# A new written-out order for an attention-then-mixer kernel, with half the scores of six more head pairs masked in SBUF

## The chip, the cores and the metric

The kernel runs on one core of one Trainium2 chip. A core has a matrix engine (TensorE, PE in the profile), a vector engine (VectorE, DVE), a scalar engine (ScalarE, ACT), GpSimd (POOL), and SyncE (SP), which here only issues transfers. Each engine works through its own list of instructions in the order in which they were written, and waits on semaphores for the others. Matmuls write to PSUM, which has eight banks; everything else lies in SBUF. The metric is the device time of one execution in microseconds.

## What is computed

The reference has two parts. The first is linear attention with a decay per head, over 4 batches, 8 heads, 768 positions and head size 64. It goes in blocks of 64 positions:

```
intra = (q_block @ k_block.T) * Dmask          # Dmask[i, j] = lam**(...) for i >= j, else 0
out   = intra @ v_block + (q_block * lam_pow) @ kv_state
kv_state = lam**64 * kv_state + (k_block * rev_pow).T @ v_block
```

The second part takes the heads side by side as x (4 x 768 x 512) and mixes the tokens:

```
W_tok = (x @ w_q) @ (x @ w_k).T / sqrt(64)     # per batch, 768 x 768
out   = relu(W_tok @ x) @ w_out
```

## The kernel before, in words

**Tiles.** Heads go two at a time: a *pair* n is batch n // 4 and heads 2(n % 4) and 2(n % 4) + 1, so there are 16 pairs, four to a batch. Positions go in six chunks of 128. All data are bf16 on the chip; the inputs are f32 in memory and are cast by the load.

**Pieces of a pair.** Each pair passes through a fixed set of pieces. On TensorE: `Aq` and `Ak` turn q and k by 12 transposes each (L251, L260); `S0` and `S1` make the scores of chunks 0 to 2 and 3 to 5 (six matmuls each, L277); `P` makes the running sums of k times v (10, L319); `I` multiplies q by these (10, L347) and `V` adds scores times v (12, L359), both into the same two banks; `F` turns the result (six, L382). Between them stand copies out of PSUM: `eq` (VectorE, also multiplies by the decay, L266), `ek`, `G`, `ex` and `ef`, each on ScalarE or VectorE as the order says (L234; `G` of pairs from 6 on is three VectorE instructions, L335 to L337). `sv` multiplies v by its decay, in SBUF, on VectorE or GpSimd (L239).

**Masks.** The scores have to be multiplied by a mask of ones and zeros. `M0` and `M1` (L291) do this on VectorE straight out of PSUM. For half the scores of pairs 0 to 3 the old order has two steps instead: `Mc` (L306) copies the unmasked scores to SBUF on ScalarE, and `Mm` (L310) multiplies them there by the mask, on VectorE, both operands lying in SBUF.

**Pieces of a batch.** Once the four `ef` of a batch b are there: `Q` (two halves, L404; for batch 0 in eight parts `Qp`, L414), `eQ`, `K` (L430; `Kh` in batch 0), `eK`, `Y` (L455), the three copies `YA`, `YB`, `YC` out of one bank, four `m` (two matmuls each, L479), their relu copies `em` (or halves, `eh`, L490 on ScalarE and L492 on VectorE), and six `O` (four matmuls of 512 columns, L508) with copies `eo`, each followed by a store of 256 KB that SyncE issues (L519). `Z` are matmuls on zeros that nobody reads (L528).

**What sets the order.** No scheduler runs when the kernel is built. A text, `ORDER`, names the pieces one after the other, and a loop at the end (L540) issues them. A word such as `ek.5@1:v` is piece `ek` of pair 5 on PSUM bank 1, on VectorE (`:a` ScalarE, `:p` GpSimd). Pieces with two banks use the named one and the next. So one text fixes the list of every engine, and the bank of every piece; a piece that writes a bank waits until the copy that read the bank's previous contents is done. GpSimd's list holds the loads of q, k and v, one pair after another, with nine of the sixteen `sv` between them. `hold` makes SyncE wait for k of pair 14 before its first store.

The text was found by a search that planned with costs and landing times; the search itself is not part of the kernel. The loop that issues it:

Of the kernel before, what the change touches and what calls it, by code (L numbers as in the profile page):

```python
# [28 lines left out]
ORDER = """  # L29
q.2 k.2 v.2 q.3 k.3 v.3 wq.0 wk.0 q.4 k.4 v.4 wo.0 q.5 k.5 v.5 q.6 k.6 v.6 q.7 k.7 v.7 sv.4:p q.8  # L30
k.8 v.8 sv.5:p q.9 k.9 v.9 q.10 k.10 v.10 sv.7:p q.11 k.11 v.11 q.12 k.12 v.12 sv.9:p q.13 k.13
v.13 sv.10:p q.14 k.14 v.14 sv.11:p q.15 k.15 v.15 sv.12:p sv.13:p sv.14:p hold.14 Aq.0@0 dq.2
eq.0@0 dq.3 Z.5@7 Ak.0@0 dq.1 ek.0@0:v Z.3@7 S1.0@0 sv.0:v S0.0@2 Mc.0@2 M1.0@0 Z.3@7 P.0@4 Aq.1@5
G.0@4:a Mm.0:v Z.1@7 I.0@0 eq.1@5 Ak.1@4 V.0@0 ek.1@4:v ex.0@0:a S0.1@4 sv.1:v S1.1@2 Mc.1@4 Z.1@7
F.0@0 M1.1@2 P.1@1 ef.0@0:a Aq.2@4 Mm.1:v G.1@1:a eq.2@4 Z.1@7 Ak.2@0 I.1@2 ek.2@0:v V.1@2 S1.2@0
sv.2:v ex.1@2:a S0.2@4 Mc.2@4 M1.2@0 Z.3@7 P.2@2 Aq.3@3 G.2@2:a Mm.2:v F.1@4 eq.3@3 Ak.3@2
ef.1@4:v I.2@0 V.2@0 ek.3@2:v ex.2@0:a sv.3:v Z.1@7 S0.3@2 S1.3@4 cw.0:a M1.3@4 Mc.3@2 Z.2@7 P.3@0
Qp.0.0@1 F.2@6 G.3@0:a Mm.3:v Qp.0.1@1 ef.2@6:a I.3@4 V.3@4 Qp.1.0@0 ex.3@4:a Aq.4@6 Ak.4@7 eq.4@6
F.3@4 ek.4@7:a Qp.1.1@0 Qp.0.2@1 eg.3.0@4:v Qp.1.2@0 eg.3.1@4:v Qp.0.3@1 eQ.0.0@1:v Qp.1.3@0
S1.4@4 eQ.0.1@0:a Kh.0.0@1 M1.4@4 ek2.0.0@1:a Kh.0.1@0 S0.4@6 ek2.0.1@0:a M0.4@6 Y.0@0 YA.0@0:a  # L40
YB.0@0:v Aq.5@1 YC.0@0:a m.0.1@6@7 eq.5@1 m.0.0@4@5 eh.0.1.0@6:a eh.0.0.0@4:v eh.0.0.1@5:a Ak.5@1
eh.0.1.1@7:a m.0.2@4@6 ek.5@1:v m.0.3@5@0 eh.0.2.1@6:a eh.0.3.1@0:v S0.5@2 eh.0.3.0@5:a S1.5@6
eh.0.2.0@4:v P.4@0 O.0.5@5 G.4@0:v M1.5@6 I.4@0 eo.0.5@5:a V.4@0 M0.5@2 Aq.6@4 ex.4@0:a Ak.6@5
eq.6@4 O.0.4@6 ek.6@5:a sv.6:v S1.6@4 S0.6@0 M1.6@4 F.4@7 O.0.3@2 ef.4@7:a M0.6@0 P.5@3 eo.0.3@2:a
Ak.7@7 G.5@3:v Aq.7@0 ek.7@7:a P.6@2 eq.7@0 I.5@4 V.5@4 G.6@2:v S0.7@0 ex.5@4:a eo.0.4@6:v Aq.8@7
M0.7@0 I.6@2 S1.7@4 O.0.0@6 eq.8@7 M1.7@4 V.6@2 eo.0.0@6:a O.0.2@7 ex.6@2:a sv.8:v P.7@6
eo.0.2@7:a Ak.8@2 G.7@6:v P.8@3 ek.8@2:a F.5@7 G.8@3:v Aq.9@6 ef.5@7:a Ak.9@2 eq.9@6 S1.8@4
ek.9@2:a S0.8@0 I.7@6 M1.8@4 V.7@6 F.6@2 ex.7@6:a M0.8@0 O.0.1@3 ef.6@2:v F.7@6 eo.0.1@3:a Aq.10@7
ef.7@6:v S0.9@2 eq.10@7 S1.9@0 Ak.10@6 M1.9@0 Q.1.0@7 ek.10@6:a M0.9@2 Q.1.1@4 eQ.1.0@7:a I.8@6
eQ.1.1@4:a S1.10@0 P.9@5 M1.10@0 K.1@4 V.8@6 eK.1@4:a G.9@5:v Aq.11@2 ex.8@6:a Y.1@4 eq.11@2  # L50
Ak.11@5 YA.1@4:a YB.1@4:v S0.10@2 ek.11@5:v YC.1@4:a m.1.0@6 M0.10@2 em.1.0@6:a m.1.1@0 Aq.12@5
P.10@4 em.1.1@0:a eq.12@5 m.1.3@2 I.9@6 G.10@4:v em.1.3@2:a V.9@6 m.1.2@0 ex.9@6:v I.10@4
em.1.2@0:a F.8@2 V.10@4 ef.8@2:v S0.11@0 ex.10@4:a S1.11@6 M0.11@0 O.1.1@2 M1.11@6 F.9@3
eo.1.1@2:a O.1.0@0 ef.9@3:a Ak.12@2 eo.1.0@0:a P.11@3 ek.12@2:v Ak.13@1 Aq.13@0 G.11@3:v ek.13@1:a
S1.12@6 S0.12@4 eq.13@0 I.11@2 V.11@2 M0.12@4 O.1.4@0 ex.11@2:a M1.12@6 F.10@1 eo.1.4@0:a F.11@2
ef.10@1:a S0.13@6 ef.11@2:v S1.13@4 Ak.14@0 M1.13@4 P.13@1 ek.14@0:a Aq.14@2 G.13@1:v Q.2.0@3
eq.14@2 Q.2.1@0 eQ.2.0@3:a M0.13@6 S1.14@2 eQ.2.1@0:a I.13@4 O.1.5@1 M1.14@2 V.13@4 sv.15:v
eo.1.5@1:a P.14@0 ex.13@4:a Aq.15@2 G.14@0:v K.2@1 Ak.15@3 eK.2@1:a P.12@4 eq.15@2 P.15@0
ek.15@3:a Y.2@1 G.12@4:v G.15@0:v S0.14@4 YB.2@1:a S0.15@2 I.12@6 YA.2@1:a M0.14@4 V.12@6 YC.2@1:a
O.1.2@0 ex.12@6:a M0.15@2 S1.15@4 eo.1.2@0:a I.14@6 m.2.1@2 M1.15@4 F.12@1 em.2.1@2:a V.14@6  # L60
ef.12@1:a I.15@4 ex.14@6:v m.2.2@2 V.15@4 em.2.2@2:a F.13@0 ex.15@4:v F.14@1 ef.13@0:a m.2.0@2
m.2.3@6 ef.14@1:v F.15@4 em.2.0@2:a O.1.3@0 ef.15@4:v em.2.3@6:a Q.3.0@1 eo.1.3@0:a Q.3.1@6
eQ.3.0@1:a O.2.0@0 eQ.3.1@6:v K.3@1 eo.2.0@0:v O.2.4@6 eK.3@1:a Y.3@7 eo.2.4@6:a O.2.3@6 YA.3@7:v
YB.3@7:v YC.3@7:v m.3.1@0 eo.2.3@6:a O.2.2@4 em.3.1@0:a m.3.0@6 eo.2.2@4:a m.3.2@2 m.3.3@0
em.3.0@6:v O.2.5@5 em.3.2@2:a em.3.3@0:a O.2.1@4 eo.2.5@5:v O.3.0@0 eo.2.1@4:a O.3.2@1 eo.3.0@0:v
O.3.4@4 eo.3.2@1:a O.3.3@5 eo.3.4@4:v O.3.1@1 eo.3.3@5:a O.3.5@0 eo.3.1@1:a eo.3.5@0:a
"""


# [506 lines left out]
```

## Time and profile before

| | |
|---|---|
| time, median of 11 runs | 99.17 us (98.59 to 100.45) |
| time of the profiled execution | 99.17 us |
| its span, first to last instruction | 97.4 us |
| PE busy, with a matmul in flight | 90.1 us |
| DVE, ACT, POOL busy | 72.2, 61.5, 61.5 us |
| granted TensorE clock, mean | 0.992 |
| POOL's last multiply of v ends | 65.74 us |
| last load (v of pair 15) landed | 66.98 us |
| PE's last matmul starts | 92.97 us |
| the last copy out of PSUM | 93.43 to 94.01 us |
| last store landed | 96.09 us |

All times within the execution count from the span's start. The rows of the profile name an engine, the line of the kernel, the operation, what it writes and reads, how often it occurs, its busy time and the mean duration of one instruction in nanoseconds, and then how long the engine stood idle just before. A matmul's row lasts from its issue to the end of its passage through the array, so rows of neighbouring matmuls overlap and their durations do not add up to time; the distance from one start to the next does.

### The profile page before, as it was taken

The numbers are of one execution on the slowest core, as the hardware profiler recorded it, in microseconds if no ns is written. First come the engines' busy times: TensorE is split into PE (matmuls) and PEld (weight loads), VectorE is DVE, ScalarE is ACT, GpSimd is POOL, SyncE is SP. The second block draws the span as 40 slices with busy tenths as digits, with TensorE's granted clock in tenths as the row PEclk, the third lists the DMA queues.
The fourth block names the chain that finished last, engine by engine and source line by source line (L and its number), as shares of the span: only waits on it lengthen the run. The fifth ranks groups of instructions, "written<-read, shape, count | busy, mean of one in ns | idle before, by whom it ended". The sixth has DMA issues, their size and how long they took to land.

```text
span 97.4 us, 3425 instructions
## 1 busy us (share of the span) xinstructions
PE 90.1 (93%) x1469; PEld 56.6 (58%) x1469; DVE 72.2 (74%) x140; ACT 61.5 (63%) x101; POOL 61.5 (63%) x65
## 2 busy tenths in 40 slices
...
GB/s 1 88 137 158 164 158 169 155 165 186 191 159 167 168 158 168 164 160 167 166 161 167 164 165 163 172 169 369 395 312 18 108 7 108 215 170 215 284 306 102
DMA packets 67438, 16.60 MB, mean 170 GB/s; under 512 B 63840, under 2 KB 64352, under 8 KB 67424
## 3 DMA queue, kind: packets, MB, share of 16 engines
...
## 4 chain that ended last, share of the span: by engine, by line
PE 67%; POOL 10%; DMA 8%; DVE 6%; ACT 3%; issue 2%; POOLq 0%; DVEq 0%; ACTq 0%
PE ps L508 21%; DMA fk<-in_k_dram 8%; PE ps L359 6%; PE ps L277 5%; PE ps L260 5%; PE ps L382 5%; PE ps L404 4%; PE ps L251 4%; PE ps L319 4%; POOL fq L113 3%; PE ps L455 3%; POOL fk L117 3%; POOL fv L121 3%; PE ps L347 3%; DVE pr L291 3%; PE ps L479 2%
## 5 line engine op out<-in xcount | busy, mean ns | idle before, releaser
L291 DVE TENSOR_TENSOR pr<-ps,mask 128x768 bf16<-128x768 f32 x28 | 25.9, 950 | 0.8 <-PE ps L277 0.7
L508 PE MATMUL ps<-wo,rmT 128*128 128x512 bf16 x96 | 23.6, 380 | 0.0
L117 POOL DMA_DIRECT2D fk<-in_k_dram x16 | 16.8, 1048 | 1.5 <-DMA wo<-in_moe_w_out_dram 1.5
L234 ACT COPY osb<-ps 128x512 f32<-128x512 f32 x19 | 11.2, 589 | 10.0 <-PE ps L508 8.9
L121 POOL DMA_DIRECT2D fv<-in_v_dram x16 | 16.8, 1052 | 0.3 <-issue 0.3
L113 POOL DMA_DIRECT2D fq<-in_q_dram x16 | 14.2, 884 | 1.3 <-POOLq L560 0.8
L234 ACT CAST xnat<-ps 128x768 bf16<-128x768 f32 x13 | 10.4, 800 | 6.8 <-PE ps L359 6.5
L239 POOL TENSOR_TENSOR fv<-fv,DvI 128x768 bf16<-128x768 bf16 x9 | 13.4, 1507 | 0.0
L508 PEld LDWEIGHTS <-rmT 128*128 128x128 bf16 x96 | 8.3, 98 | 8.6 <-issue 0.7
L528 PE MATMUL ps<-blank 128*128 128x512 bf16 x29 | 10.4, 481 | 1.2 <-DVE blank L158 1.2
L266 DVE TENSOR_TENSOR qT<-ps,dq 128x768 bf16<-128x768 bf16 x16 | 8.9, 554 | 2.7 <-PE ps L251 2.4
L490 ACT ACTIVATE rmT<-ps 128x768 bf16<-128x768 f32 (+1 forms) x16 | 10.6, 721 | 0.2
L277 PE MATMUL ps<-qT,kT 64*128 64x128 bf16 x192 | 9.0, 218 | 0.4 <-DVE kT L234 0.3
L234 ACT COPY kT<-ps 128x768 bf16<-128x768 bf16 x9 | 7.2, 800 | 2.9 <-PE ps L260 2.4
L251 PE MATMUL ps<-ident,fq 128*64 128x128 bf16 x192 | 8.6, 227 | 0.2
L260 PE MATMUL ps<-ident,fk 128*64 128x128 bf16 x192 | 8.3, 221 | 0.5 <-DMA fk<-in_k_dram 0.3
L359 PE MATMUL ps<-fv,pr 128*128 128x64 bf16 x192 | 8.5, 194 | 0.1
L277 PEld LDWEIGHTS <-kT 64*128 64x128 bf16 x192 | 5.6, 94 | 4.0 <-DVE kT L234 1.4
L319 PE MATMUL ps<-fv,fk 128*64 128x128 bf16 (+4 forms) x160 | 7.8, 229 | 0.0
L382 PE MATMUL ps<-order,xnat 128*128 128x128 bf16 x96 | 7.8, 220 | 0.0
L359 PEld LDWEIGHTS <-pr 128*128 128x128 bf16 x192 | 6.8, 98 | 1.5 <-issue 0.4
L251 PEld LDWEIGHTS <-fq 128*64 128x64 bf16 x192 | 6.3, 113 | 2.3 <-DMA fq<-in_q_dram 1.1
...
## 6 DMA issues: line engine op xcount, KB each, us to landing
...
lam_all<-in_lam_dram SPq DMA_DIRECT2D x1, 4.0 KB, 2.5
```

Source lines behind the costliest of these rows:

```text
L113: nc.gpsimd.dma_start(out=fq[n], in_=rows_q(n))
L117: nc.gpsimd.dma_start(out=fk[n], in_=rows(n, k))
L121: nc.gpsimd.dma_start(out=fv[n], in_=rows(n, v))
L234: return (nc.scalar.copy if eng == "a" else nc.vector.tensor_copy)(out=to, in_=of)
L239: (nc.gpsimd if eng == "p" else nc.vector).tensor_tensor(out=vn[n], in0=fv[n], in1=DvI[:, 2 * kk : 2 * kk + 2, :].unsqueeze(3).to_broadcas ...
L251: nc.tensor.transpose(to.rearrange("e (t r p) -> e r t p", t=2, r=2)[:, r], fq[n][:, hl, a, r * D : (r + 1) * D], ident,)
L260: nc.tensor.transpose(PSH[R[hl], o, c * CH : (c + 1) * CH], fk[n][:, hl, c, :], ident)
L277: mm(PS[:, o + hl, cc * CH : (cc + 1) * CH], kT[n][R[hl], c], qT[n][R[hl], c], start=True, stop=True, skip_group_check=True,)
L291: nc.vector.tensor_tensor(out=pr[n, a].rearrange("j l (c i) -> j l c i", c=3), in0=PS[:, o : o + 2, 0:HALF].rearrange("j l (c i) -> j l c ...
L359: mm(PS[:, o + hl, c * D : (c + 1) * D], pr[n, c // 3][:, hl, (c % 3) * CH : (c % 3 + 1) * CH], vn[n][:, hl, c, :], start=False, stop=(c = ...
L382: nc.tensor.transpose(PSH[:, o, c * CH : (c + 1) * CH], xnat[b][:, c, kk * CH : (kk + 1) * CH], order,)
L508: mm(PS[:, o, :], rmT[b][:, kt].rearrange("f n i -> f (n i)")[:, t * CH : (t + 1) * CH], wo[:, kt, :], start=(kt == 0), stop=(kt == 3),)
```

## The change

Only `ORDER` changes, and with it every engine's list except GpSimd's and SyncE's, which issue the same things in the same order. Line numbers below the text move by one. In the new text

- pairs 10 to 15 get `Mc` and `Mm` for half of their scores too (half 0), so VectorE has six `M0` fewer and six `Mm` more, and ScalarE six `Mc` more;
- copies change between ScalarE and VectorE (for example `ek.8` to VectorE and `eo.0.4` to ScalarE), and pieces change places and banks;
- the number of `Z` matmuls goes from 29 to 31, counting nine ahead of the order;
- TensorE changes the shape of its part of the array (128*128, 128*64 or 64*128 rows by columns) 93 times in place of 101.

The diff, with the parts left out that the text does not speak of:

```
-eq.0@0 dq.3 Z.5@7 Ak.0@0 dq.1 ek.0@0:v Z.3@7 S1.0@0 sv.0:v S0.0@2 Mc.0@2 M1.0@0 Z.3@7 P.0@4 Aq.1@5
...
-YB.0@0:v Aq.5@1 YC.0@0:a m.0.1@6@7 eq.5@1 m.0.0@4@5 eh.0.1.0@6:a eh.0.0.0@4:v eh.0.0.1@5:a Ak.5@1
-eh.0.1.1@7:a m.0.2@4@6 ek.5@1:v m.0.3@5@0 eh.0.2.1@6:a eh.0.3.1@0:v S0.5@2 eh.0.3.0@5:a S1.5@6
-eh.0.2.0@4:v P.4@0 O.0.5@5 G.4@0:v M1.5@6 I.4@0 eo.0.5@5:a V.4@0 M0.5@2 Aq.6@4 ex.4@0:a Ak.6@5
...
-eQ.1.1@4:a S1.10@0 P.9@5 M1.10@0 K.1@4 V.8@6 eK.1@4:a G.9@5:v Aq.11@2 ex.8@6:a Y.1@4 eq.11@2
-Ak.11@5 YA.1@4:a YB.1@4:v S0.10@2 ek.11@5:v YC.1@4:a m.1.0@6 M0.10@2 em.1.0@6:a m.1.1@0 Aq.12@5
...
-ef.10@1:a S0.13@6 ef.11@2:v S1.13@4 Ak.14@0 M1.13@4 P.13@1 ek.14@0:a Aq.14@2 G.13@1:v Q.2.0@3
-eq.14@2 Q.2.1@0 eQ.2.0@3:a M0.13@6 S1.14@2 eQ.2.1@0:a I.13@4 O.1.5@1 M1.14@2 V.13@4 sv.15:v
-eo.1.5@1:a P.14@0 ex.13@4:a Aq.15@2 G.14@0:v K.2@1 Ak.15@3 eK.2@1:a P.12@4 eq.15@2 P.15@0
...
+M1.1@4 Z.2@7 P.1@0 Aq.2@1 G.1@0:a Mm.1:v F.0@2 eq.2@1 I.1@4 Ak.2@0 ef.0@2:v V.1@4 ek.2@0:v
+ex.1@4:a Z.1@7 S1.2@0 S0.2@2 M1.2@0 Mc.2@2 F.1@4 sv.2:v ef.1@4:a Z.2@7 Aq.3@5 eq.3@5 Z.1@7 P.2@4
+Mm.2:v Ak.3@2 G.2@4:v ek.3@2:a sv.3:v Z.4@7 S1.3@2 cw.0:a S0.3@4 I.2@0 M1.3@2 Mc.3@4 P.3@6 V.2@0
...
+Aq.5@6 YA.0@7:a YB.0@7:v eq.5@6 YC.0@7:a m.0.1@4@5 eh.0.1.0@4:a eh.0.1.1@5:v m.0.3@7@2 m.0.0@6@3
+eh.0.3.1@2:a eh.0.3.0@7:v Ak.5@1 eh.0.0.1@3:a ek.5@1:v P.4@7 eh.0.0.0@6:a G.4@7:v S1.5@0 m.0.2@6@3
+S0.5@4 eh.0.2.0@6:a M1.5@0 Aq.6@2 eh.0.2.1@3:a I.4@6 V.4@6 eq.6@2 O.0.4@3 M0.5@4 ex.4@6:a O.0.5@2
...
+Q.1.0@7 eq.9@4 Q.1.1@6 eQ.1.0@7:v S1.9@4 eQ.1.1@6:a S0.9@2 I.8@0 M1.9@4 K.1@6 Ak.10@7 eK.1@6:a
+M0.9@2 P.9@4 ek.10@7:a Y.1@6 G.9@4:v Aq.11@7 YB.1@6:a YA.1@6:a eq.11@7 YC.1@6:a m.1.0@4 m.1.1@2
+em.1.0@4:a m.1.2@6 em.1.1@2:v V.8@0 em.1.2@6:a m.1.3@4 Aq.12@2 ex.8@0:a Ak.11@3 eq.12@2 Aq.10@6
+em.1.3@4:a ek.11@3:v Ak.12@7 eq.10@6 S0.11@2 S1.11@4 ek.12@7:v I.9@0 Mc.11@2 V.9@0 M1.11@4 O.1.1@7
+ex.9@0:a Mm.11:v P.10@6 eo.1.1@7:a S0.10@0 G.10@6:v S1.10@4 Mc.10@0 F.8@7 M1.10@4 F.9@2 ef.8@7:a
+O.1.2@6 Mm.10:v ef.9@2:a O.1.0@7 eo.1.2@6:a I.10@2 eo.1.0@7:a S0.12@4 P.11@6 Mc.12@4 Ak.13@7
+G.11@6:v Aq.13@0 V.10@2 eq.13@0 P.12@6 ex.10@2:v S1.12@0 I.11@4 V.11@4 G.12@6:v F.10@2 ex.11@4:a
+O.1.5@3 Mm.12:v M1.12@0 ef.10@2:a F.11@6 O.1.4@4 eo.1.5@3:a ef.11@6:v ek.13@7:v Q.2.1@6 eo.1.4@4:a
+sv.15:v Q.2.0@7 P.13@4 eQ.2.0@7:a eQ.2.1@6:v Ak.14@5 Aq.15@3 G.13@4:v ek.14@5:a K.2@2 P.14@6
+eq.15@3 Ak.15@4 eK.2@2:a G.14@6:v Aq.14@5 ek.15@4:a S0.13@2 eq.14@5 S1.13@0 I.12@6 Mc.13@2 M1.13@0
+V.12@6 S1.15@4 ex.12@6:a S0.15@2 Mm.13:v Y.2@0 Mc.15@2 M1.15@4 P.15@1 I.13@6 YA.2@0:a S1.14@2
+G.15@1:v YB.2@0:a S0.14@4 V.13@6 Mc.14@4 YC.2@0:v O.1.3@1 M1.14@2 ex.13@6:a I.14@4 Mm.14:v m.2.2@2
+eo.1.3@1:a I.15@6 Mm.15:v V.14@4 em.2.2@2:a V.15@6 ex.14@4:v F.13@1 ex.15@6:a F.12@0 ef.13@1:v
+F.14@4 F.15@5 ef.12@0:v ef.14@4:a m.2.1@6 ef.15@5:v m.2.3@0 m.2.0@2 em.2.1@6:a Q.3.1@5 em.2.0@2:v
+em.2.3@0:a Q.3.0@4 eQ.3.1@5:a O.2.2@0 eQ.3.0@4:v K.3@1 eo.2.2@0:a O.2.0@4 eK.3@1:v Y.3@5
+eo.2.0@4:v O.2.5@1 YA.3@5:a YB.3@5:v YC.3@5:v m.3.0@2 eo.2.5@1:v m.3.1@4 m.3.2@6 em.3.0@2:a
...
```

More of the change, by code (lines that the diff above doesn't have):

```diff
@@ L31 @@
 k.8 v.8 sv.5:p q.9 k.9 v.9 q.10 k.10 v.10 sv.7:p q.11 k.11 v.11 q.12 k.12 v.12 sv.9:p q.13 k.13
-v.13 sv.10:p q.14 k.14 v.14 sv.11:p q.15 k.15 v.15 sv.12:p sv.13:p sv.14:p hold.14 Aq.0@0 dq.2
-eq.0@0 dq.3 Z.5@7 Ak.0@0 dq.1 ek.0@0:v Z.3@7 S1.0@0 sv.0:v S0.0@2 Mc.0@2 M1.0@0 Z.3@7 P.0@4 Aq.1@5
-G.0@4:a Mm.0:v Z.1@7 I.0@0 eq.1@5 Ak.1@4 V.0@0 ek.1@4:v ex.0@0:a S0.1@4 sv.1:v S1.1@2 Mc.1@4 Z.1@7
-F.0@0 M1.1@2 P.1@1 ef.0@0:a Aq.2@4 Mm.1:v G.1@1:a eq.2@4 Z.1@7 Ak.2@0 I.1@2 ek.2@0:v V.1@2 S1.2@0
-sv.2:v ex.1@2:a S0.2@4 Mc.2@4 M1.2@0 Z.3@7 P.2@2 Aq.3@3 G.2@2:a Mm.2:v F.1@4 eq.3@3 Ak.3@2
@@ L37 @@
[L37 to L40, printed above, removed]
-YB.0@0:v Aq.5@1 YC.0@0:a m.0.1@6@7 eq.5@1 m.0.0@4@5 eh.0.1.0@6:a eh.0.0.0@4:v eh.0.0.1@5:a Ak.5@1
-eh.0.1.1@7:a m.0.2@4@6 ek.5@1:v m.0.3@5@0 eh.0.2.1@6:a eh.0.3.1@0:v S0.5@2 eh.0.3.0@5:a S1.5@6
@@ L43 @@
-eh.0.2.0@4:v P.4@0 O.0.5@5 G.4@0:v M1.5@6 I.4@0 eo.0.5@5:a V.4@0 M0.5@2 Aq.6@4 ex.4@0:a Ak.6@5
[L44 to L48, printed above, removed]
@@ L49 @@
-ef.7@6:v S0.9@2 eq.10@7 S1.9@0 Ak.10@6 M1.9@0 Q.1.0@7 ek.10@6:a M0.9@2 Q.1.1@4 eQ.1.0@7:a I.8@6
-eQ.1.1@4:a S1.10@0 P.9@5 M1.10@0 K.1@4 V.8@6 eK.1@4:a G.9@5:v Aq.11@2 ex.8@6:a Y.1@4 eq.11@2
-Ak.11@5 YA.1@4:a YB.1@4:v S0.10@2 ek.11@5:v YC.1@4:a m.1.0@6 M0.10@2 em.1.0@6:a m.1.1@0 Aq.12@5
-P.10@4 em.1.1@0:a eq.12@5 m.1.3@2 I.9@6 G.10@4:v em.1.3@2:a V.9@6 m.1.2@0 ex.9@6:v I.10@4
-em.1.2@0:a F.8@2 V.10@4 ef.8@2:v S0.11@0 ex.10@4:a S1.11@6 M0.11@0 O.1.1@2 M1.11@6 F.9@3
-eo.1.1@2:a O.1.0@0 ef.9@3:a Ak.12@2 eo.1.0@0:a P.11@3 ek.12@2:v Ak.13@1 Aq.13@0 G.11@3:v ek.13@1:a
@@ L55 @@
-S1.12@6 S0.12@4 eq.13@0 I.11@2 V.11@2 M0.12@4 O.1.4@0 ex.11@2:a M1.12@6 F.10@1 eo.1.4@0:a F.11@2
-ef.10@1:a S0.13@6 ef.11@2:v S1.13@4 Ak.14@0 M1.13@4 P.13@1 ek.14@0:a Aq.14@2 G.13@1:v Q.2.0@3
-eq.14@2 Q.2.1@0 eQ.2.0@3:a M0.13@6 S1.14@2 eQ.2.1@0:a I.13@4 O.1.5@1 M1.14@2 V.13@4 sv.15:v
-eo.1.5@1:a P.14@0 ex.13@4:a Aq.15@2 G.14@0:v K.2@1 Ak.15@3 eK.2@1:a P.12@4 eq.15@2 P.15@0
-ek.15@3:a Y.2@1 G.12@4:v G.15@0:v S0.14@4 YB.2@1:a S0.15@2 I.12@6 YA.2@1:a M0.14@4 V.12@6 YC.2@1:a
-O.1.2@0 ex.12@6:a M0.15@2 S1.15@4 eo.1.2@0:a I.14@6 m.2.1@2 M1.15@4 F.12@1 em.2.1@2:a V.14@6
@@ L61 @@
[L61 to L66, printed above, removed]
+v.13 sv.10:p q.14 k.14 v.14 sv.11:p q.15 k.15 v.15 sv.12:p sv.13:p sv.14:p hold.14 Aq.0@0 dq.1
@@ new lines @@
+eq.0@0 dq.3 Z.5@7 Ak.0@0 dq.2 ek.0@0:v Z.3@7 S1.0@0 sv.0:v S0.0@2 Mc.0@2 M1.0@0 Z.3@7 P.0@4 Aq.1@5
+G.0@4:a Mm.0:v Z.1@7 I.0@0 eq.1@5 Ak.1@4 V.0@0 ek.1@4:v ex.0@0:a S1.1@4 sv.1:v S0.1@2 Mc.1@2
+M1.1@4 Z.2@7 P.1@0 Aq.2@1 G.1@0:a Mm.1:v F.0@2 eq.2@1 I.1@4 Ak.2@0 ef.0@2:v V.1@4 ek.2@0:v
+ex.1@4:a Z.1@7 S1.2@0 S0.2@2 M1.2@0 Mc.2@2 F.1@4 sv.2:v ef.1@4:a Z.2@7 Aq.3@5 eq.3@5 Z.1@7 P.2@4
+Mm.2:v Ak.3@2 G.2@4:v ek.3@2:a sv.3:v Z.4@7 S1.3@2 cw.0:a S0.3@4 I.2@0 M1.3@2 Mc.3@4 P.3@6 V.2@0
+G.3@6:a Mm.3:v Qp.1.0@7 ex.2@0:a I.3@2 V.3@2 Aq.4@6 ex.3@2:a F.2@0 eq.4@6 Qp.0.0@1 F.3@2 ef.2@0:v
```

10 lines of the change are left out of this document (added).

## The prediction

> **What bounds the kernel now.** I read the page's head and slices first, then sums by stretch, then the chain, then single rows.
>
> ```profile
> span 97.4 us, 3425 instructions
> PE 90.1 (93%) x1469; PEld 56.6 (58%) x1469; DVE 72.2 (74%) x140; ACT 61.5 (63%) x101; POOL 61.5 (63%) x65
> ...
> L291 DVE TENSOR_TENSOR pr<-ps,mask 128x768 bf16<-128x768 f32 x28 | 25.9, 950 | 0.8 <-PE ps L277 0.7
> ```
>
> ```profile
> 31.50:45.00 13.50, 13.45 (x260) 9.05 (x257) 12.97 (x24) 7.74 (x13) 13.50 (x14) 1.00 2.26 165
> 45.00:59.10 14.10, 13.41 (x292) 10.04 (x289) 11.97 (x22) 9.98 (x17) 14.10 (x14) 1.00 2.26 164
> 59.10:67.00 7.90, 7.90 (x162) 5.72 (x158) 6.62 (x12) 5.73 (x9) 6.64 (x6) 1.00 2.13 195
> 67.00:78.00 11.00, 11.00 (x235) 7.96 (x234) 10.67 (x23) 8.96 (x17) 0.00 (x0) 1.00 0.61 229
> ```
>
> (Columns: stretch, length, then busy time and count of PE, PEld, DVE, ACT, POOL; clock; DMA.) PE is busy nearly all the time, at full clock, so its order sets the end. But two others run close to it: POOL is full until 65.7, and DVE has 10.67 of the 11.00 us from 67 to 78. A busy PE hides small waits, because a matmul lasts about 200 ns and pipelines. So I took each piece's pitch, from its start to the next one's, and the chain shows what sets it:
>
> ```profile
> 39.29 0.46 PE ps L359 x12
> 40.98 0.97 PE ps L508 x4
> 41.95 0.35 PE ps L359 x12
> 42.30 0.86 PE ps L508 x4
> 43.54 0.34 PE ps L260 x12
> ```
>
> The same V piece takes 0.35 or 0.46, the same O piece 0.86 or 0.97. The longer one stands where the next piece uses another shape of the array: 128*128 (V, F, Q, O), 128*64 (Aq, Ak, P, K, Y) or 64*128 (S0, S1, I, m). I call this a **shape change**; it costs 0.097 us.
>
> Pitches without it, from the starts in the trace: Aq, Ak 0.34; S0, S1, m 0.17; I 0.165; P 0.256 (0.438 for pairs below 6); V 0.348; F 0.336; O 0.863; Q 0.655; K 0.19; Y 0.665. From P.4 on (start 31.55) the old order has 24 O, 12 P, 12 I, 12 V, 12 F, 12 m, 20 turns (Aq, Ak), 20 halves of scores, 6 Q, 3 K and 3 Y = 53.07 us, and 60 changes = 5.82: 58.89 of work left. 31.55 + 58.89 = 90.44; the last O really ends its issue at 92.32 + 0.86 = 93.18. So waits after P.4 cost 2.74: 2.30 of it before O.1.1 (start 59.15, 33.59 left), 0.13 up to Q.2.0 (66.87, 26.00 left), 0.31 in the rest.
>
> **The change, part by part.** Work before P.4: two dummy matmuls more (Z, 0.43) and other places for the first pairs. Both orders are held there by the same landings. POOL's list is unchanged, so loads and its multiplies keep their times. Ak.3 waits for k.3 (landed 19.13, Ak.3 at 19.17), and new P.1 to P.2 reach that point at about 19.2 too. Then P.4 waits for POOL's multiply of v.4:
>
> ```profile
> 29.81 1.48 POOL L239 TENSOR_TENSOR fv<-fv,DvI 128x768 bf16<-128x768 bf16 x1
> ```
>
> It ends at 31.29. The old P.4 came 0.26 later, behind S0.5 and S1.5; in the new order P.4 stands ahead of S1.5, m.0.2 and S0.5 and waits for it: 31.35. The dummies therefore cost nothing; without that cover 0.43.
>
> *Work after P.4*: the same pieces, plus those three (0.51), with 56 changes (5.43): 59.01. 31.35 + 59.01 = 90.36, so 0.08 better than before, with no wait counted.
>
> *P.4 to O.1.1.* I walked the new lists with the rows' durations (start of a copy 0.04 after the matmuls' ends, PE 0.055 after a copy's end). PE waits: 0.1 at I.4 for a relu half; 0.28 at P.7 for POOL's sv.7 (ends 42.82); 0.06 at Q.1.0; 0.24 at P.9, whose bank M1.9 reads; 0.58 at m.1.0 (after Y.1 stands only Aq.11, 0.44, against 0.88 to Y's last result and 0.37 each for YB and YA, one behind the other on one bank); 0.23 at m.1.2 to Aq.12; 0.19 at S0.11 for ek.11; 0.1 in smaller ones: 1.8. O.1.1 at 57.2 with 34.98 left: 92.2, against 92.74 before.
>
> *Masking pairs 10 to 15 late.* Each M0 on DVE (0.95, net 0.865, since DVE instructions overlap 0.083) becomes an ACT copy Mc (0.80) and an Mm on DVE (0.55, net 0.465). DVE gains 6 x 0.40 = 2.4 us; ACT is charged 6 x 0.70 = 4.2 net, in a stretch where it has 14.7 of 18.9 us filled. Mm reads both inputs from SBUF. The trace has four of them, all before POOL's first multiply:
>
> ```profile
> L310 DVE TENSOR_TENSOR pr<-pr,mask x4: 549/550/557, 10.4 to 22.3; 128x768 bf16<-128x768 bf16 x4
> ```
>
> The new Mm.11 and Mm.12 fall on POOL's multiplies (the rows: sv.11, and sv.12 to sv.14 until 65.74):
>
> ```profile
> 57.07 1.50 POOL L239 TENSOR_TENSOR fv<-fv,DvI 128x768 bf16<-128x768 bf16 x1
> ...
> 61.40 4.35 POOL L239 TENSOR_TENSOR fv<-fv,DvI 128x768 bf16<-128x768 bf16 x3
> ```
>
> By the row Mm.12 costs 0.55 there. The Trainium skill ("SBUF — State Buffer", Who interferes with whom) says that a DVE instruction with two SBUF inputs contends with a GpSimd instruction that reads SBUF, and that whoever issues first keeps the port for the whole instruction. The nearest row is a DVE multiply of v, also with two SBUF inputs, which met POOL's sv.5 (34.14 to 35.65):
>
> ```profile
> 34.80 1.67 DVE L239 TENSOR_TENSOR fv<-fv,DvI 128x768 bf16<-128x768 bf16 x1
> ```
>
> 1.67 in place of 0.95: 0.72 lost of 0.84 overlapped. So I take the rule. In the walk ex.10 ends at 64.5, G.12 at 65.1, and Mm.12 follows: by the row it ends 65.6, by the rule (0.64 overlapped, 85% lost) 66.2. Behind it on DVE stand M1.12 and ef.11, then ek.13, and Q.2.1 needs ef.11 and its bank: 66.2 + 0.87 + 0.47 + 0.06 = 67.6, where PE would be there at 67.0. By the row O.1.1's 92.2 grows to 92.3 (Ak.13 and F.10 wait 0.1); by the rule to 92.9. Bounds: 0 and 0.9 (Mm.12 as early as sv.14's start). Mm.11 loses the same way and has slack.
>
> *Q.2.1 to the end.* From Q.2.1 to Q.3.1 PE has 25.30 - 13.98 = 11.32 us. DVE's list from sv.15 to ef.15, which Q.3.1 needs, net: sv 0.865; eQ.2.1, ek.14, eq.15, eq.14, ef.13, ef.12, ef.15 at 0.475; three Mm 1.395; three M1 2.595; three G 2.04; YC 0.34; ex.14 0.87 = 11.43. Before, DVE had 11.55 from G.13 to ef.15 against 12.02 of PE, and started level. Now sv.15 starts 0.34 after Q.2.1, 0.14 is needed at the end, and ex.14 waits 0.2 for V.14: PE loses some 0.85 (I.12 waits for G.14 0.26, Y.2 for M1.13 0.19, V.15 for Mm.15 0.12, Q.3.1 for ef.15 0.12, the rest smaller). sv.15 itself is free: v.15 landed at 66.98. Then m.3.0 and m.3.2 wait 0.15 for YC.3, behind YA and YB. Together 1.0, against 0.31 before.
>
> **Sum:** 90.36 + 1.8 + 0.1 + 0.6 + 1.0 = 93.9 against 93.18: 0.75 later. The last copy and store are the same kind in both. The profiled execution took 99.17 (97.4 of span, 1.77 around it), equal to the median of the eleven runs: **99.9**. What a measurement of this kernel can tell from no change is about 0.3%, 0.3 us.
>
> **Rivals.**
> *No lock:* Mm.12 runs 0.55 beside POOL, or starts after 65.74, and the rest is as above. 93.3: 99.3. For it: no Mm beside a multiply is in the trace. Against it: the 1.67 row.
>
> *DVE relieved, faster:* the 2.4 us freed make DVE early in the last stage. The price is decided at G.14, M1.13 and ef.15: if DVE is 0.26 us earlier there than I count, those waits go, and there is no lock either: 92.3 + 0.3 = 92.6, 98.6. It also needs P.12 at 63.4 as walked; POOL's sv.12 (62.90) + 28.83 left allows no end below 91.8. Against it: 11.43 against 11.32.
>
> *ACT becomes the bound around batch 1:* from K.1 to S1.11 PE has 4.84 us; ACT's list (eK, ek.10, YB, YA, YC, three em, ex.8) is 4.7 net and starts 0.4 after K.1. Each wait then passes to the next, m.1.0 first; with lock and DVE as forecast and another 0.9 here: 100.8. For it: the 0.58 is already there. Against it: DVE shares these copies.
>
> **How the numbers follow.** Forecast 0.48 (its own range 99.5 to 100.4), no lock 0.20, relieved 0.12, ACT 0.20. The range takes in part of the rivals on both sides: 98.7 to 101.3 takes in the ACT case with half a us more, and leaves out the better half of the relieved one. Faster by over 0.3% (below 98.87): 0.12. Within: 0.22 (no lock, and the forecast's low edge). Slower: 0.66.
>
> **What would show it.** P.4 starting at about 31.35 right at POOL's end; m.1.0 waiting over 0.4 us for YA; Mm.12 over 1 us long, or not (lock step); Q.2.1 at 67.0 or 67.6; DVE without idle time from sv.15 to Mm.15 and PE waiting on G.14 and M1.13; the late masks of pairs 13 to 15 at 0.55 each. Wrong it would be if POOL's times move, since everything is hung on them, or if PE's pitches differ at the new shape changes.

## The result, and the profile after

| | before | after |
|---|---|---|
| median, measured side by side | 99.59 us (50 runs) | 100.84 us (13 runs, 100.64 to 101.07) |
| ratio, with its 95% interval | | 1.0142 (1.0119 to 1.0165) |
| profiled execution, its span | 99.17, 97.4 us | 101.27, 99.5 us |

The changed kernel is slower by 1.4%. The forecast was 99.9, 0.75 above the profiled execution of before; the medians differ by 1.25. The ratio makes it 1.4, because it leaves out executions over 1.5% above the fastest of their kernel, which are nine of the 50 of before and none of the changed one. So the sign and the range held, and the increase was half a microsecond too small. Another 0.42 of the distance to 100.84 is the base: beside the changed kernel, before ran at 99.59 and not at 99.17.

The page of the changed kernel, the rows that answer to those of before:

```profile
span 99.5 us, 3429 instructions
...
PE 88.7 (89%) x1471; PEld 56.3 (57%) x1471; DVE 76.4 (77%) x149; ACT 60.5 (61%) x98; POOL 61.6 (62%) x65
...
L509 PE MATMUL ps<-wo,rmT 128*128 128x512 bf16 x96 | 23.2, 379 | 0.6 <-DVE gs L338 0.6
L292 DVE TENSOR_TENSOR pr<-ps,mask 128x768 bf16<-128x768 f32 x22 | 20.7, 952 | 1.5 <-PE ps L278 1.4
```

Six masks out of PSUM went (28 to 22 rows), yet VectorE is busy 4.2 us longer than before (76.4 against 72.2), and an O piece of TensorE now waits 0.6 us for a VectorE copy, `gs`.

The sums by stretch, cut where the same pieces start in the new order (P.4, O.1.1, Q.2.1, Q.3.1; columns as before):

```profile
31.90:45.00 13.10, 12.99 (x248) 8.78 (x247) 11.55 (x20) 7.68 (x13) 13.10 (x13) 1.00 2.25 164
45.00:57.70 12.70, 11.98 (x275) 9.15 (x275) 11.25 (x23) 9.29 (x16) 12.70 (x14) 1.00 2.27 164
57.70:68.33 10.63, 10.00 (x173) 6.61 (x169) 9.12 (x19) 7.67 (x12) 8.73 (x7) 1.00 2.00 220
68.33:80.50 12.17, 12.00 (x272) 9.22 (x271) 11.59 (x25) 10.30 (x17) 0.00 (x0) 1.00 0.48 181
```

In the last of them VectorE is nearly full (11.59 of 12.17 us) and ScalarE has little left (10.30). The clock is 1.00, so no loss is the clock's.

Where the time went is read with the prediction's own measure: the start of a piece plus the pitches of all pieces still to come. A rise from one piece to the next is waiting in between.

| start + work left | predicted | before | after | rise, after less before |
|---|---|---|---|---|
| P.4 | 90.36 | 90.44 | 90.91 | +0.47 |
| O.1.1 | 92.2 | 92.73 | 92.70 | -0.50 |
| Q.2.1 | 92.9 | 92.87 | 93.63 | +0.79 |
| end of TensorE's issue | 93.9 | 93.18 | 94.83 | +0.89 |
| last store landed | +2.91 | 96.09 | 98.22 | +0.48 |

The first rise comes from the loads of this one execution. POOL's list ran 0.55 late in it, because an early issue waited for the load of v.2, whose last part landed at 17.64, where before it landed at 15.92. The issue in POOL's timeline, with the wait in front of it:

```profile
17.92 1.01 POOL L122 DMA_DIRECT2D fv<-in_v_dram  x1 [1.58 <-DMA fv<-in_v_dram]
```

Its multiply of v.4 began at 30.36. In six of the runs below v.2 landed at 15.9 to 16.1 and that multiply began at 29.8 to 30.0, as before (29.81). In the five executions where v.2 landed at 17.14 to 17.64, this one among them, it began 12.69 to 12.72 after the landing: the delay is passed on whole. Other loads can delay it too: the run that moves P.4 began it at 30.16, with v.2 on time, after a longer wait for the load of w_out (1.70 us against 1.51 before), and the combined one at 30.61, with v.1 a microsecond late. Three other rises remain: one before Q.2.1, one behind it, one at the last stores.

*Before Q.2.1.* The chain of waits of the changed kernel runs through the mask of pair 11 in SBUF:

```profile
57.56 0.95 DVE pr L292
58.51 1.81 DVE pr L311
60.97 1.89 PE ps L509 x8
```

`Mm.11`, and `Mm.10` after it, in VectorE's timeline:

```profile
58.42 1.90 DVE L311 TENSOR_TENSOR pr<-pr,mask 128x768 bf16<-128x768 bf16 x1
...
61.70 0.54 DVE L311 TENSOR_TENSOR pr<-pr,mask 128x768 bf16<-128x768 bf16 x1
```

GpSimd's timeline, the multiply of v.11:

```profile
57.62 1.51 POOL L240 TENSOR_TENSOR fv<-fv,DvI 128x768 bf16<-128x768 bf16 x1
```

`Mm.11` took 1.90 us in place of 0.55. `G.10` stands right behind it on VectorE, and O.1.2 needs the bank that `G.10` reads: it waited 0.80, which is all but 0.13 of the rise from O.1.1 to Q.2.1.

*Behind Q.2.1.* TensorE waited at S0.15 (0.14), m.2.2 (0.27), V.15 (0.12), F.14 (0.07), Q.3.1 (0.11), m.3.2 and O.2.3 (0.14 each), and less elsewhere: 1.20 together, against 0.31 before.

*The last stores.* From TensorE's end to the issue of the last store it took 0.86 in both kernels. The store itself took 2.06 us before and 2.53 now. (The stores follow their copies, so SyncE's list is not the same as before: its last store is that of O.3.1 in place of O.3.5. Both have 256 KB.) The page of the changed kernel has one more transfer of instructions (q14) and a later median landing of the stores (eleven early ones take over 4 us beside the loads, so three late ones more move the median):

```profile
q14 instruction: 4, 0.03, 0.1%
...
out_dram<-osb SPq DMA_DIRECT2D x24, 256.0 KB, 2.6
```

Before:

```profile
q14 instruction: 3, 0.02, 0.1%
...
out_dram<-osb SPq DMA_DIRECT2D x24, 256.0 KB, 2.1
```

### The profile page after: what moved, and what is told of

It is laid out like the page before. It is cut to its first block, busy times and chain, and to the rows that moved or that the text cites. A ratio compares the mean times of both kernels' runs of the same rounds, so it can differ in the third digit from the quotient of the medians.

```text
span 99.5 us, 3429 instructions
## 1 busy us (share of the span) xinstructions
PE 88.7 (89%) x1471; PEld 56.3 (57%) x1471; DVE 76.4 (77%) x149; ACT 60.5 (61%) x98; POOL 61.6 (62%) x65
## 4 chain that ended last, share of the span: by engine, by line
PE 35%; POOL 24%; DMA 17%; DVE 14%; issue 3%; ACT 2%; POOLq 0%; ACTq 0%; DVEq 0%
PE ps L509 16%; DMA wo<-in_moe_w_out_dram 9%; DMA fv<-in_v_dram 9%; POOL fk L118 7%; POOL fv L122 7%; POOL fq L114 5%; POOL fv L240 5%; PE ps L405 4%; DVE pr L292 4%; PE ps L320 2%; PE ps L360 2%; DVE pr L311 2%; PE ps L480 2%; DVE qT L267 2%; DVE xT L235 2%
## 5 line engine op out<-in xcount | busy, mean ns | idle before, releaser
L292 DVE TENSOR_TENSOR pr<-ps,mask 128x768 bf16<-128x768 f32 x22 | 20.7, 952 | 1.5 <-PE ps L278 1.4
L235 ACT CAST xnat<-ps 128x768 bf16<-128x768 f32 x14 | 11.2, 801 | 8.1 <-PE ps L360 8.1
L235 ACT COPY osb<-ps 128x512 f32<-128x512 f32 x16 | 9.4, 588 | 8.4 <-PE ps L509 8.2
L491 ACT ACTIVATE rmT<-ps 128x768 bf16<-128x768 f32 (+1 forms) x15 | 9.6, 685 | 2.4 <-PE ps L480 2.3
L529 PE MATMUL ps<-blank 128*128 128x512 bf16 x31 | 9.8, 434 | 1.2 <-DVE blank L159 1.2
L307 ACT CAST pr<-ps 128x768 bf16<-128x768 f32 x10 | 8.0, 803 | 1.2 <-PE ps L278 1.1
L235 DVE COPY osb<-ps 128x512 f32<-128x512 f32 x8 | 5.5, 691 | 4.1 <-PE ps L509 4.1
L320 PEld LDWEIGHTS <-fk 128*64 128x64 bf16 x160 | 6.3, 110 | 3.7 <-issue 2.3
L240 DVE TENSOR_TENSOR fv<-fv,DvI 128x768 bf16<-128x768 bf16 x7 | 7.6, 1087 | 0.8 <-DMA fv<-in_v_dram 0.7
```

Source lines behind the costliest of these rows:

```text
L235: return (nc.scalar.copy if eng == "a" else nc.vector.tensor_copy)(out=to, in_=of)
L240: (nc.gpsimd if eng == "p" else nc.vector).tensor_tensor(out=vn[n], in0=fv[n], in1=DvI[:, 2 * kk : 2 * kk + 2, :].unsqueeze(3).to_broadcas ...
L292: nc.vector.tensor_tensor(out=pr[n, a].rearrange("j l (c i) -> j l c i", c=3), in0=PS[:, o : o + 2, 0:HALF].rearrange("j l (c i) -> j l c ...
L320: mm(to[R[hl], c:end, :], fk[n][:, hl, c, :], vn[n][:, hl, c, :].unsqueeze(1).to_broadcast([128, end - c, D]), start=(c == 0), stop=(c == ...
L529: mm(PS[:, o, :], blank[:, 0:128], blank, start=True, stop=True)
```

## The experiments

The theory after the result had three parts: a mask in SBUF that is held beside POOL costs the rise before Q.2.1; VectorE's list costs the one behind it; a fetch of instructions delays the last stores. All kernels but the last two start from the changed one; those two build on the combined order. Each ratio is to the kernel before, run beside it (median 99.68, for the runs with M0 for pair 10 99.51, for P.15 early 99.64). A loss between two pieces is, as above, the rise of start plus work left.

### Are held masks the loss before Q.2.1?

M0 in place of Mc and Mm, first for pair 11, then for pairs 11 and 12:

```diff
-I.9@0 Mc.11@2 V.9@0 M1.11@4
+I.9@0 M0.11@2 V.9@0 M1.11@4
-ex.9@0:a Mm.11:v P.10@6
+ex.9@0:a P.10@6
```

> Changed kernel with the late mask of pair 11 alone undone: M0.11 on VectorE in place of Mc.11 and Mm.11. In the changed kernel Mm.11 took 1.90 us beside GpSimd's multiply sv.11 and O.1.2 waited 0.8 us for G.10 behind it. Lock theory: that wait goes, TensorE reaches Q.2.1 earlier, and now Mm.12 starts before sv.14 ends (66.4) and is held in turn (over 0.9 us long), so only some 0.2 to 0.4 us of the 0.8 is kept: about 100.5. Rival (DVE is simply late there, a longer M0 is as bad): O.1.2 still waits over 0.5 us, Mm.12 stays at 0.55, time 100.8 or more.

Measured: 100.94, ratio 1.0118 (1.0078 to 1.0158). The time is not told apart from the changed kernel's (1.0142). O.1.2's wait is gone and O.1.1 to O.1.2 loses 0.24 in place of 0.83, but Mm.10 and Mm.12, which follow, start earlier and are held in their turn:

```profile
60.51 1.76 DVE L311 TENSOR_TENSOR pr<-pr,mask 128x768 bf16<-128x768 bf16 x1
...
65.54 1.34 DVE L311 TENSOR_TENSOR pr<-pr,mask 128x768 bf16<-128x768 bf16 x1
```

Q.2.1 now waits 0.75, and its start plus work left is 93.57 against 93.63, although P.4 came 0.54 earlier here, with v.2 on time: the loss has moved 7 us down the list.

> The late masks of pairs 11 and 12 both undone (M0.11 and M0.12), the other four kept. Lock theory: no SBUF mask is left beside a GpSimd multiply of v, O.1.2's wait goes and nothing takes its place; Q.2.1 starts at about 67.6 in place of 68.33, time 100.84 - 0.7 = 100.1. Rival (DVE's amount of work decides): DVE gets 0.8 us more work, time 100.8 to 101.2.

Measured: 100.5, ratio 1.0075 (1.005 to 1.01). All masks in SBUF take their short time (the line's summary: shortest, median, longest in ns):

```profile
L311 DVE TENSOR_TENSOR pr<-pr,mask x8: 547/548/558, 10.2 to 76.5; 128x768 bf16<-128x768 bf16 x8
```

The time is 0.34 below the changed kernel by the medians, 0.65 by the ratios; 0.7 was expected. Q.2.1 starts at 67.57, where the forecast had 67.6, with 92.87 (before 92.87), but that is luck: 0.51 of the 0.76 gained there is P.4, which had v.2 on time. From O.1.1 to Q.2.1 this order still loses 0.68, against 0.93 in the changed kernel, and 0.67 or 0.68 in all seven runs with M0 for both pairs. M0 is not free in these places. VectorE's row of M0.11 and M1.11:

```profile
57.05 1.81 DVE L292 TENSOR_TENSOR pr<-ps,mask 128x768 bf16<-128x768 f32 x2
```

S1.10 waits 0.20 for the bank that M1.11 reads, P.12 0.16 for `G.11` behind M0.12, S1.12 0.11 and F.10 0.10 for the next two copies. Three more executions below have the changed order up to Q.2.1: they lose 0.87, 1.28 and 1.33, with Mm.11 held for 1.84, 2.25 and 2.30. So the hold is the wait at O.1.2, and M0 wins back 0.2 to 0.65 of it. What these masks would cost in SBUF without a hold, no run shows.

### What does the start hang on?

P.4 and G.4 put behind S1.5, m.0.2 and S0.5, so that TensorE has work while POOL multiplies v.4:

```diff
-P.4@7 eh.0.0.0@6:a G.4@7:v S1.5@0 m.0.2@6@3
-S0.5@4 eh.0.2.0@6:a
+eh.0.0.0@6:a S1.5@0 m.0.2@6@3
+S0.5@4 P.4@7 G.4@7:v eh.0.2.0@6:a
```

> Changed kernel with P.4 and G.4 moved three pieces later, behind S1.5, m.0.2 and S0.5, as in the kernel before. In the changed kernel P.4 waits 0.82 us for GpSimd's sv.4 (ends 31.85) with these pieces (0.5 us) standing behind it. Pin theory: TensorE does them in the wait, everything after P.4 comes 0.4 to 0.5 us earlier at first; GpSimd's later multiplies (sv.7 at P.7) and the lock at Mm.11 take part of it back, since they are tied to GpSimd's times: 100.4 to 100.7. Rival (wait only moves): 100.84.

Measured: 101.6, ratio 1.0195 (1.015 to 1.0239). That is 0.8 above the changed kernel and missed by both readings. P.4's wait became one of 0.75 at S1.5 for `ek.5` and one of 0.32 at I.4, whose `G.4` now comes later. Two engines deliver at the same time there; work can't be drawn ahead of one without meeting the other. These waits don't make up the whole 0.8: O.1.1 comes 0.2 to 0.35 later than in most of the runs with v.2 on time. The rest is open.

### What sets the stage behind Q.2.1?

All six late masks undone (M0 again for pairs 10 to 15; the edit of pair 13, the others are alike):

```diff
-Mc.13@2
+M0.13@2
-Mm.13:v
```

> Changed kernel with the late masks of all six pairs 10 to 15 undone (M0 in place of Mc, the six Mm dropped), all else as in the changed order. Lock theory: no SBUF mask beside a GpSimd multiply, so O.1.2 and Q.2.1 come as in e2_m11_m12 (Q.2.1 about 67.6). Late-stage theory (VectorE works without a gap from G.13 to Mm.15, 7.5 us, against 7.5 of TensorE from P.13 to V.15): three M0 in place of three Mm add 1.2 us to that stretch, TensorE waits 0.8 to 1.2 more there than in e2, time 101.2 to 101.6. Rival (ScalarE, also without a gap there, sets it): ScalarE loses 2.1 us, the waits shrink, time 100.0 to 100.4.

Measured: 102.43, ratio 1.0295 (1.0236 to 1.0353), slower than either reading allowed. Up to Q.2.1 it is as with M0 for 11 and 12 (92.99); behind it TensorE loses 3.3 us, and it is VectorE's masks that it waits for (who waited for this line, us, times):

```profile
  PE ps L480: 1.0, 1
  PE ps L456: 0.5, 1
  PE ps L278: 0.5, 2
```

So this order needs the late masks of pairs 13 to 15: they save 2 us behind Q.2.1, where POOL no longer multiplies (0.55 each), while those of pairs 11 and 12 cost where it does. The question is what the remaining 1.20 is. The prediction said VectorE's list, from sv.15 to ef.15. First sv.15 on GpSimd, 0.865 less on VectorE:

```diff
-v.15 sv.12:p sv.13:p sv.14:p hold.14
+v.15 sv.12:p sv.13:p sv.14:p sv.15:p hold.14
-sv.15:v Q.2.0@7
+Q.2.0@7
```

> Changed kernel with the multiply of v of pair 15 on GpSimd, behind its last one, in place of VectorE. Theory of the last stage (VectorE's list from sv.15 to ef.15, 11.4 us, is longer than TensorE's 11.3 from Q.2.1 to Q.3.1): VectorE has 0.87 us less, the waits of TensorE there (0.9 in the changed kernel) fall by 0.4 to 0.7, time 100.2 to 100.4. Rival (these waits come from short distances between a copy and its reader, not from the amount): they stay, 100.8.

Measured: 101.44, ratio 1.0173 (1.0148 to 1.0199). From Q.2.1 to Q.3.1 TensorE loses 0.82, as before the edit, at the same pieces. VectorE used the gain to stand idle 0.54 us before `G.13`, which waits for TensorE's P.13. The list does not begin at sv.15, and the rival held: the waits stay. The time is 0.6 above the changed kernel's; in this execution Mm.11 was held for 2.25 us and the last store took 2.85, but whether the timed ones have the same is not known.

Then the three masks of pairs 13 to 15 left out, 1.4 us less on VectorE behind `G.13`; the scores of their first halves stay unmasked, so the output is another:

```diff
-Mm.13:v
-Mm.14:v
-Mm.15:v
```

> Leaves out Mm.13, Mm.14 and Mm.15: half of the scores of these three pairs stay unmasked, so the output is another one; nothing else changes. VectorE theory: the gapless stretch G.13 to Mm.15 loses 1.4 us, TensorE's waits at m.2.2 (0.27) and V.15 (0.12) go, 100.4 or less. Rival (ScalarE's gapless stretch from ek.14 to em.2.2, or short distances, set the stage): waits stay at S0.15, F.14 and Q.3.1 and m.2.2 keeps most of its own, 100.7 to 100.9.

Measured: 100.97, ratio 1.0138 (1.0077 to 1.0199). Q.2.1 to Q.3.1 loses 0.79. V.15's wait is gone, F.14's grew from 0.07 to 0.27, m.2.2's fell only from 0.27 to 0.22. VectorE now stands idle 1.1 us at a stretch, before `ex.14`, which waits for TensorE's V.14, and the stage loses as much. VectorE's amount of work is not the cause.

Last, P.15 ahead of Y.2 on TensorE, in the order of the run "M0.10 too" below, which has Mm.13 and Mm.15 on GpSimd. There `G.15` had waited 0.33 for P.15, and m.2.2 0.22 for the bank that M1.14 reads behind `G.15` and YC (the three took 2.13 us, not 2.28):

```diff
-Y.2@0 Mc.15@2 M1.15@4 P.15@1 I.13@6
+P.15@1 Y.2@0 Mc.15@2 M1.15@4 I.13@6
```

> The run with M0.10 too, and on TensorE P.15 ahead of Y.2 instead of behind it, with as many shape changes. There VectorE stood idle 0.33 us before G.15 for P.15 and then ran G.15, YC and M1.14 in 2.28 us, and m.2.2 waited 0.22 for the bank that M1.14 reads. Short-distance theory (one chain through VectorE, not the amount of work on either engine): G.15 starts without idle time, m.2.2 starts without a wait, and the loss from Q.2.1 to Q.3.1, start plus work left, falls from 0.77 to about 0.55; time 99.9 to 100.0. Full-lists theory (ScalarE has no gap there): the same amount comes back at I.15, V.15, F.14 or Q.3.1, the loss stays at 0.7 to 0.8; time 100.1 to 100.2.

Measured: 100.18, ratio 1.0073 (1.0046 to 1.0101). `G.15` starts at once, and VectorE then waits 0.52 at YC, for ScalarE's YB:

```profile
73.57 0.35 DVE L338 TENSOR_TENSOR gs<-ps,two 128x192 bf16<-128x192 f32 x1
74.44 0.43 DVE L235 CAST YB<-ps 64x256 bf16<-64x256 f32 x1 [0.52 <-ACT YB L235]
74.89 0.96 DVE L292 TENSOR_TENSOR pr<-ps,mask 128x768 bf16<-128x768 f32 x1
```

TensorE's Y.2, then ScalarE's Mc.15, YA, YB and Mc.14 in the same execution:

```profile
72.77 0.85 PE L456 MATMUL ps<-xnat,wkn 128*64 128x256 bf16 x12
```

```profile
72.74 0.83 ACT L307 CAST pr<-ps 128x768 bf16<-128x768 f32 x1
73.66 0.37 ACT L235 CAST YA<-ps 128x256 bf16<-128x256 f32 x1
74.04 0.36 ACT L235 CAST YB<-ps 64x256 bf16<-64x256 f32 x1
74.43 0.80 ACT L307 CAST pr<-ps 128x768 bf16<-128x768 f32 x1
```

Q.2.1 to Q.3.1 loses 0.84 and m.2.2 waits 0.28, so the numbers are those of the full-lists reading. Its cause is not what the trace shows. ScalarE was done with Mc.15 at 73.57, Y.2 ended at 73.62, and YA began at 73.66: it waited for TensorE. Moving P.15 forward had put Y.2 back by 0.26, and its three copies run one after the other, all out of one bank: YA to 74.03, YB from 74.04 to 74.40, YC from 74.44. One chain, P.15, `G.15`, YC, M1.14, m.2.2, was exchanged for another that ends no sooner, Y.2, YA, YB, YC, M1.14, m.2.2. F.14 waits 0.19 in the same way, for V.14's copy, before which VectorE stood idle:

```profile
76.94 0.96 DVE L235 CAST xnat<-ps 128x768 bf16<-128x768 f32 x1 [0.62 <-PE ps L360]
```

Q.3.1 (0.11) waits for `ef.15`, which starts as F.15 ends. Only S0.15 (0.14) hangs on a full list: Mc.13 stands right behind `ek.15` on ScalarE. So short chains from TensorE through a copy and back are what the stage waits for once VectorE is relieved. No run removes them all, so what would win the stage back stays open.

### Is it the fetch at the last stores?

In the changed kernel the fourth q14 transfer lies at 95.84, as VectorE comes to its 192nd instruction of 195 (the trace counts semaphore waits too, the page only 149 that keep it busy), and the last three stores are under way (issued 93.97, 94.95, 95.69). Fifteen of the sixteen parts of each land as ever, 2.0 us after issue; the sixteenth comes 0.5 to 0.6 later. That q14 is VectorE's is read from its times: its 8 KB transfers lie at VectorE's 71st to 74th, 104th or 105th and 127th to 129th instruction in every run and, where its list goes on beyond that, at its 190th to 193rd. Before, the same transfer lay at 98.13, behind the last store. Four late copies of O put on ScalarE leave VectorE with 187 instructions:

```diff
-eo.2.1@1:v
-eo.2.4@0:v
-eo.3.3@0:v
-eo.3.2@2:v
+eo.2.1@1:a
+eo.2.4@0:a
+eo.3.3@0:a
+eo.3.2@2:a
```

> Four of the last copies of output (eo.2.1, eo.2.4, eo.3.2, eo.3.3) on ScalarE in place of VectorE, nothing else. In the changed kernel the last three stores landed 2.5 to 2.7 us after their issue began, against 2.05 before; only the last of their 16 parts was late, and an 8 KB fetch of instructions ran at 95.8, when VectorE had come to its 192nd instruction. Fetch theory: VectorE stays four instructions short of it, the fetch falls behind the last store, which lands 2.05 after its issue: 0.4 to 0.5 us less, 100.4. Rival (stores are slowed by the spacing of the last copies or by chance): they still take 2.4 or more, 100.8.

Measured: 100.96, ratio 1.0137 (1.0079 to 1.0195). The profile did what the theory said: the transfer lies at 100.67, and the last three stores land 2.04 to 2.05 us after issue. The time did not show it (1.0142 for the changed kernel); in the profiled execution Mm.11 was held for 2.30 us and O.1.2 waited 1.19. With held masks out of the way, the same edit was tried again, as a pair (M0 for pairs 10, 11 and 12; without and with these four copies):

> M0 for pairs 10, 11 and 12 alone; the last copies of O as in the changed kernel. Lock theory: as with M0 for 11 and 12 (100.5), 100.2 to 100.5, since Mm.10 was not held there in its profile; last three stores 2.4 to 2.7 us after issue. If Mm.10 is held in other executions: up to 0.3 less, 99.9 to 100.2.

> M0 for pairs 10, 11 and 12 and the four late copies of O on ScalarE; the masks of pairs 13 to 15 stay on VectorE in SBUF. Instruction-fetch theory of the tail: VectorE ends with about 187 instructions, no fetch among the last stores, all three landed 2.0 to 2.1 us after issue, and the time is 0.4 to 0.5 us below the run with M0 alone. Rival (the lateness of the last parts is seen in profiled executions only, or the copies on ScalarE cost as much): within 0.15 us of that run.

Measured: without, 100.7, ratio 1.0119 (1.0086 to 1.0151), last stores 2.26 to 2.45 us; with, 100.36, ratio 1.0087 (1.0058 to 1.0116), last stores 2.04 to 2.06 us. The medians differ by 0.34, which is less than the 0.4 to 0.5 expected and more than the rival's 0.15; the intervals overlap, so its size is known only roughly. A third M0, for pair 10, gave nothing: 1.0119 against 1.0075 for pairs 11 and 12 alone.

Moving copies also changes their spacing. A run above settles that rival: with all six late masks undone the transfer lies at 93.03, the four copies are still on VectorE, and the last four stores land in 2.02 to 2.10 us, while the three under way at 93.03 take 2.46 to 2.78 and the next one 2.35. In all fourteen executions the stores under way at that transfer are the late ones, and where it comes well ahead of the last ones or behind them, these take 2.02 to 2.10.

### Together

M0 for 11 and 12, Mm.13 and Mm.15 on GpSimd, the four copies of O on ScalarE, and sv.7 ahead of q.10 on GpSimd (P.7 no longer waits). The parts of the edit not shown yet:

```diff
-q.9 k.9 v.9 q.10 k.10 v.10 sv.7:p q.11
+q.9 k.9 v.9 sv.7:p q.10 k.10 v.10 q.11
-Mm.13:v
+Mm.13:p
-Mm.15:v
+Mm.15:p
```

> All that the reasons call for, at once: M0.11 and M0.12 as in e2 (0.3 to 0.7 less), the four copies of e8 (0.45 less if the fetch theory holds), Mm.13 and Mm.15 on GpSimd, which is idle then (0.3 less if VectorE is what holds the late stage), and sv.7 three loads earlier in GpSimd's list (P.7's wait of 0.28 goes). If all hold: 100.84 - 1.8 = 99.0 to 99.4, at or below the kernel before. If only e2's part holds: 100.5.

Measured: 100.06, ratio 1.003 (1.0007 to 1.0053). The best of the variants, 0.8 below the changed kernel, where 1.8 was expected, and still not below before. The parts had promised too much: M0 gave 0.34 and the four copies 0.34 in their own runs, P.7's wait is 0.3, and the masks on GpSimd, aimed at VectorE's amount, took only 0.05 off the loss from Q.2.1 to Q.3.1 (0.77). Mm.10 was held in it (1.81 us), so M0 was put in for pair 10 too:

> The combined order, with M0.10 in place of Mc.10 and Mm.10 as well, so that no mask in SBUF lies beside a POOL multiply or a DMA issue. Lock theory: in the combined run's profile Mm.10 was held for 1.81 us; with it gone O.1.1 comes to 92.2 and Q.2.1 to at most 92.9 (there 93.3), start plus work left, and the last three stores land 2.0 to 2.1 us after their issue; 99.5 to 99.8, level with before. Rival (the remaining loss is the short distances of the late stage, and the hold of Mm.10 had slack): 100.0 to 100.2, as the combined order.

Measured: 100.16, ratio 1.0078 (1.0049 to 1.0107): the rival's 100.0 to 100.2. O.1.1 to Q.2.1 loses 0.67 with and without the hold of Mm.10, so that one had slack. O.1.1 and Q.2.1 reach 91.98 and 92.65, 0.75 and 0.2 better than before. Behind Q.2.1 TensorE again loses 1.20 (TensorE's end 93.86), against 0.31 before. It is this stage that keeps the order from the kernel before: without its 0.9 more, this execution would end 0.2 ahead.

## Why the prediction was right and where it was wrong

**P.4 pinned by POOL's v.4: right.** 90.36 predicted; 90.34 to 90.52 in the six runs with the same order there whose v.2 landed by 16.1. The 90.91 of the profiled execution is the late v.2, not the order.

**The waits from P.4 to O.1.1: right.** Walked 1.8, measured 92.70 - 90.91 = 1.79, and at the places named: P.7 0.29 (0.28), P.9 0.23 (0.24), m.1.0 0.57 (0.58), S0.11 0.20 (0.19). At I.4 it was 0.04 in place of 0.1. ScalarE as the bound at batch 1, one of the rivals, fell with this: m.1.0 waited its 0.57, and the further 0.9 did not come.

**The lock: right in kind, wrong in place and price.** The step that failed is "Mm.11 loses the same way and has slack". It was priced at 85% of its overlap, about 0.6 us; it lost 1.35 for 0.71 of overlap, and the slack was not walked through: `G.10`, then O.1.2, 0.80. Late by this, VectorE came to Mm.12 at 66.36, as POOL's last multiply ended (66.43), and Mm.12 took 0.55. So the charge of 0.6 fell at the other mask and was 0.8. Once Mm.11 was out (the first run) Mm.12 was held after all, 1.34 us, and Q.2.1 waited 0.75 there. The rate of 85% was right for it (0.79 lost of 0.93, behind GpSimd's last multiply). It failed for Mm.11, which was held on beyond the multiply (last section).

**Behind Q.2.1: right in size, wrong in cause.** 1.0 predicted, 1.20 measured, at S0.15, m.2.2, V.15 and Q.3.1 rather than at I.12 and Y.2. The step that failed is "11.43 against 11.32", VectorE's list longer than TensorE's. It counted `ek.14` on VectorE, where the order gives it to ScalarE; without it the list is 10.95 and shorter than TensorE's, and it began at sv.15, which has slack in front of `G.13`. Taking 0.87 or 1.4 us off VectorE left the loss at 0.82 and 0.79. The runs show chains of single copies in its place (m.2.2, F.14, Q.3.1) and 0.14 at S0.15 from ScalarE's list. That a sum with a wrong item came so near the size is luck.

**The end: missed.** "The last copy and store are the same kind in both" is true, and the store was 0.47 us longer all the same in the profile; 0.34 in the pair of timed runs. The prediction compared copies and not the count of VectorE's instructions.

**Sum.** Against before, without the late v.2: P.4 -0.03 (90.41, the mean of the six runs), waits to O.1.1 -0.50, to Q.2.1 +0.79, behind it +0.89, the stores +0.48: +1.63 in profiles, 1.25 in medians. (The profiled execution is one, and slower than all 13 timed ones.) Predicted: -0.08, -0.5, +0.57, +0.69 and nothing for the stores, which is 0.7, in its own rounding 0.75. The largest term that the forecast lacked is the stores, which it put at nothing (0.48 in the profile, 0.34 in the pair); the masks and the stage behind Q.2.1 were 0.2 each more than it said. The rival "no lock" fell with the 1.90 row, "VectorE relieved" with the fact that relieving it brings nothing.
